# Weights converted ahead during MLP 1 and kept in DRAM, and full-height score matmuls for the first pair, in a fused attention, MLP and SoLU-MLP kernel

## The chip, the cores and the metric

The kernel runs on one core of one Trainium2 chip, as one launch. The metric is device time in microseconds. The kernel before took 1009.99 us (median of 3 runs, 1005.29 to 1010.61). Its profiled execution took 1004.9 us, of which 1003.1 us lie between its first and last instruction (the span).

## The reference

Three layers follow one another, in float32 results from inputs that numpy hands over partly in float64 (the MLP weights):

```python
# attention: q, k, v (4, 12, 448, 64)
q_n, k_n = rmsnorm(q, g_q), rmsnorm(k, g_k)          # over the 64 columns of a head
attn = softmax(q_n @ k_n.T / 8)                      # 448 x 448 per head, 48 heads
x = (attn @ v), heads side by side                   # (1792, 768)
# MLP 1: w_in (768, 2048), w_out (2048, 768)
h = x @ w_in;  x = (h * sigmoid(h)) @ w_out
# MLP 2: w_in (768, 1024), w_out (1024, 768)
h = x @ w_in;  solu = h * softmax(h)                 # softmax over the 1024 columns
ln = (solu - mean) / sqrt(var + 1e-6) * g_ln;  out = ln @ w_out
```

## The kernel before, in words

**Precision and weights.** The matmuls of both MLPs run in a 32-bit format (`F32R`) in which a value is kept as a high part and a low part. Each product is three matmuls: high with low, low with high, high with high. The weights arrive as float64, two 32-bit words each, and are converted on the chip. `stages` does that for one chunk (128 partitions x 384 weights) in eight steps: `load` (a DMA of the raw words by SP's queue into `raw`), `mag` (ACT, into `cva`), `clamp`, `shift`, `sign`, `low` (four DVE instructions, into `cva` and `cvt`), `hi` (ACT writes the high part) and `lo` (POOL writes the low part as `cvt` minus high). For the last weight matrix ACT also multiplies by `g_ln`, twice a chunk. A slab is four chunks with both parts, 12,288 bytes a partition. There are 24 slabs: 16 for MLP 1 (a `w_in` and a `w_out` for each of 8 groups of 256 hidden units) and 8 for MLP 2. The buffers `raw`, `cva` and `cvt` are threefold during the MLPs.

**Room.** Slabs live in two pools: `big` (10 places, 8 of them taken by the attention's output `xt` until MLP 1 has read it) and `big2` (2 places, odd groups). MLP 2's eight slabs fit only when the places of `xt` come free, batch by batch, in the last group of MLP 1.

**Attention.** 24 pairs of heads, each with 7 score tiles of 128 x 448. A greedy planner (`timetable`) with costs and ranks sets the order on all engines. A pair's queries are split into a high part `X` (`hq`, POOL) and a low part `lz` (`lq`). Of pair 0 (`DIRECT`) the scores of a head are two matmuls over 64 partitions and one over 128; other pairs get their operands stacked by DMAs (`Z`, `bd`). Before pair 0 come its own RMS chain (`ldk`, `sqk`, `redk`, `lnk`, `exk`, `nwk`, `sck`), the transposes `Tk`, and `hk` and `lk`, which make the high and low keys from PSUM with the gains `gsc`. `warm(n)` issues n matmuls of the identity.

**MLP 1.** 32 steps, one for a group of weights and a batch of 448 tokens: part a (36 matmuls into `hp`, then two SiLU evaluations on ACT and a difference on POOL into `gt`) and, one step later, part b (36 matmuls into six `xps` tiles, each added to the running sum `x` by one DVE instruction). Part b has six PSUM buffers, part a two.

**The order of conversions.** The programme is written out in order; each engine runs its instructions in that order. `enqueue` gives every step of a chunk a due time on a clock that advances by 1.13 for each 6 matmuls, `every` apart from chunk to chunk, and `tick` issues what is due between the matmuls. `EV` holds the spacings: 6.8 for groups 2 to 6, 2.4 for the last group, 2.1 and 2.3 for MLP 2's weights, which are queued at the four steps of the last group and run on into the first tiles of MLP 2.

**MLP 2.** 14 tiles of 128 tokens: `moe2_a` (36 matmuls into `h2`), the softmax and norm on DVE and ACT (`moe2_n`), transposes (`lp`) and `moe2_b` (48 matmuls). `split` makes high and low parts of `x`. The first `moe2_a` comes before MLP 1's last part b, and tile 0's softmax steps lie between the additions of that part on DVE.

Of the kernel before, what the change touches and what calls it, by code (L numbers as in the profile page):

```python
# [9 lines left out]
F32 = mybir.dt.float32  # L10
# [83 lines left out]
def fused_kernel(ctx: ExitStack, tc, nat, qt, gqk, w_in, w_out, w2_in, w2_out, g_ln, out):  # L94
# [13 lines left out]

    def stages(w, src, g, ph, c):

# [37 lines left out]
        def hi():  # L148
            k["hi"], k["lo"] = w()[:, 0, s], w()[:, 1, s]
            if g is None:  # L150
                nc.scalar.copy(out=k["hi"], in_=k["tf"])  # L151
            else:
                nc.scalar.activation(out=k["hi"], in_=k["tf"], func=AF.Identity, scale=g[:, c // 2:c // 2 + 1])
                if LO[ph] == "p":
                    nc.scalar.activation(out=k["tf"], in_=k["tf"], func=AF.Identity, scale=g[:, c // 2:c // 2 + 1])

        def lo():
# [43 lines left out]
    lz = [a1.tile([128, 2 * S], F32R, name=f"lz{i}") for i in range(2)]  # L201

    def constants():
# [6 lines left out]
        for t in bd + lz:  # L210
            nc.gpsimd.memset(t[:, :].bitcast(F32), 0.0)

    def gains():
        nc.sync.dma_start(out=gcol[:, :], in_=gqk)
        nc.sync.dma_start(out=gln[:, :], in_=g_ln)

# [17 lines left out]
    def attention(n):  # L234

        b, j = pairs[n]
        c, st_ = {}, {}

        def step(f):
# [112 lines left out]
        def hq():  # L352
            nc.gpsimd.tensor_scalar(out=X()[:, 0, 64:512], in0=c["qT"][:, :], scalar1=1.0, scalar2=0.0,
                                    op0=ALU.mult, op1=ALU.add)

        def lq(h):
            r = slice(64 * h, 64 * h + 64)
            en[LQE[h]].tensor_tensor(out=lz[n % 2][r, h * S:(h + 1) * S], in0=c["qT"][r, :],
                                     in1=c["X"][r, 0, 64:512].bitcast(F32), op=ALU.subtract)

# [25 lines left out]
        def mixed(h):  # L386
# [13 lines left out]
        def score(i):  # L400
            h, t = TILES[i]
            sp = c["sp"][i] = ps_s.tile([128, S], F32, name="sp", tag="sp")
            x, z = c["X"], lz[n % 2]
            if h == 2:
                mm = [(z[:, 384:512], x[:, 1, keys(0)]), (bd[n % 2][:, :], x[:, 2, keys(0)]),
                      (bd[n % 2][:, :], x[:, 1, keys(0)])]
            else:
                r, q = slice(64 * h, 64 * h + 64), 64 * h + t * 128
                mm = [(z[:, h * S + q:h * S + q + 128], x[:, 1, keys(h)])]
                if n in DIRECT:  # L410
                    mm = [(x[r, 0, 64 + q:192 + q], x[r, w, keys(h)]) for w in (1, 2)] + mm
# [150 lines left out]
    def spec(n):  # L562
# [26 lines left out]
        put("Tk", "PE", .63, LP, "sck", ["ks", ("t", "T")])  # L589
        put("hq", "p", .56, L, "ldT", "qT X")  # L590
        put("hk", "a", .57, L, "Tk", [("t", "T"), "X"])
        put("lk", "v", .66, L, "hk", [("t", "T"), "X"])
        for h in "01":
            put("lq" + h, LQE[int(h)], 1.1 if LQE[int(h)] == "p" else .7, L, "hq", "qT X lz")
            if n not in DIRECT:
                put("za" + h, "SP", moved(S), LD, "hq hk", "X Z")
                put("zb" + h, "SP", moved(S), LD, "hq lk", "X Z")
            put("b" + h, "SP", moved(0), LD, "hq", "X bd")
        for i, (h, t) in enumerate(TILES):
            s = ("sp", i)  # L600
# [66 lines left out]
    for c, f in enumerate([x[2] for x in sorted(due, key=lambda x: x[1])]):  # L667
# [370 lines left out]
```

## Time and profile before

| | us |
|---|---|
| median of 3 runs (lowest, highest) | 1009.99 (1005.29, 1010.61) |
| profiled execution | 1004.9 |
| its span | 1003.1 |
| PE busy | 982.5 |
| DVE, ACT, POOL busy | 665.6, 448.0, 407.7 |

Attention takes the first 280 us, MLP 1 runs from there to about 761 us, and MLP 2 to the end. PE is the engine to read: a wait of PE is lost time unless something later absorbs it. In a row of the timeline the bracket at the end names the idle time before the instruction and what ended it. The rows of PE show matmuls of 448 columns that start 0.2 us apart and are each shown some 0.37 us long, since they are pipelined; steps are therefore measured from start to start.

### The profile page before, as it was taken

The page shows a single profiled execution, that of the slowest core. Times are in us where ns is not written, and L with a number is a line of the kernel's source. Part 1 is how long each engine was busy: PE and PEld are TensorE (multiplying, and loading weights), DVE is VectorE, ACT ScalarE, POOL GpSimd, SP SyncE. Part 2 cuts the span into 40 slices and gives each one's busy share as a digit, 9 for nine tenths or more (in the row PEclk, how much of TensorE's full clock was granted, in tenths as well). Part 3 has the DMA queues.
Part 4 walks back from the last instruction along what each step waited for, and adds up shares of the span by engine and source line. Part 5 has one row for each costly group of instructions (what it writes and reads, how often), then busy time and mean ns, then how long its engine had stood idle before and what let it go on. Part 6 is the DMA issues. An engine that isn't in the chain of part 4 may idle for free. (4 is left out here: it accounts for less than half of the span.)

```text
span 1003.1 us, 14589 instructions
## 1 busy us (share of the span) xinstructions
PE 982.5 (98%) x5070; PEld 831.9 (83%) x5070; DVE 665.6 (66%) x1319; ACT 448.0 (45%) x1054; POOL 407.7 (41%) x577
## 2 busy tenths in 40 slices
PE   7999999999999999999999999999898999999998
PEld 5666756666789999999999999999886999989998
DVE  6899898888546555555555655989999653535431
ACT  5999989988732322222222232333554221212221
POOL 6978888878333322322332232444543110100000
PEclk9999999999999999999999999999999999999999
DMA  6776767765322121212112121344431000000001
GB/s 183 213 194 180 203 176 208 192 188 133 99 63 64 50 62 48 64 48 63 48 48 63 48 63 49 110 110 111 126 96 47 16 32 17 17 31 16 32 16 48
DMA packets 42472, 89.68 MB, mean 89 GB/s; under 512 B 8544, under 2 KB 20704, under 8 KB 42400
## 3 DMA queue, kind: packets, MB, share of 16 engines
q1 hardware_dynamic: 42400, 88.76, 31.7%
q8 instruction: 40, 0.66, 0.3%
q14 instruction: 32, 0.26, 0.1%
HBM read 61.35 MB, written 5.51 MB: 67 GB/s over the span
## 5 line engine op out<-in xcount | busy, mean ns | idle before, releaser
L729 PE MATMUL hp<-xt,slab 128*128 128x448 f32 x1152 | 242.9, 368 | 2.8 <-ACT gt L736 2.8
L752 PE MATMUL xps<-gt,slab 128*128 128x448 f32 x1152 | 241.4, 367 | 3.6 <-DVE x L758 3.6
L729 PEld LDWEIGHTS hp<-xt,slab 128*128 128x128 f32 x1152 | 217.3, 189 | 24.1 <-ACT gt L736 3.2
L752 PEld LDWEIGHTS xps<-gt,slab 128*128 128x128 f32 x1152 | 217.2, 189 | 22.7 <-DVE x L758 4.6
L163 POOL TENSOR_TENSOR slab<-cvt,slab 128x384 fp32r<-128x384 f32 x96 | 101.6, 1061 | 195.7 <-ACT slab L151 166.5
L758 DVE TENSOR_TENSOR x<-xps,x 128x448 f32<-128x448 f32 x168 | 102.8, 621 | 69.7 <-PE xps L752 69.7
L151 ACT CAST slab<-cvt 128x384 fp32r<-128x384 f32 x80 | 41.3, 516 | 224.9 <-DVE cvt L145 224.9
L737 POOL TENSOR_TENSOR gt<-gf,gt 128x448 fp32r<-128x448 f32 x64 | 74.9, 1172 | 128.8 <-ACT gt L736 95.1
L423 DVE TENSOR_SCALAR_CACHE_REDUCE sp<-sp,ms 128x448 f32<-128x448 f32 x168 | 110.3, 686 | 19.7 <-PE sp L415 19.6
L921 PE MATMUL op<-slab,lt 128*128 128x384 f32 (+2 forms) x672 | 120.8, 338 | 0.0
L921 PEld LDWEIGHTS op<-slab,lt 128*128 128x128 f32 x672 | 117.6, 188 | 2.1
L848 PE MATMUL h<-slab,xh 128*128 128x512 f32 x504 | 118.0, 392 | 0.8 <-DVE x L758 0.8
L848 PEld LDWEIGHTS h<-slab,xh 128*128 128x128 f32 x504 | 93.7, 188 | 20.0 <-issue 1.1
L459 POOL TENSOR_SCALAR p<-p,st 128x448 f32<-128x448 f32 x144 | 94.4, 665 | 28.9 <-DVE st L450 23.6
L133 DVE TENSOR_SCALAR cva<-cva 128x384 f32<-128x384 f32 x96 | 58.7, 612 | 68.1 <-ACT cva L130 68.1
L434 ACT ACTIVATE p<-sp,st 128x448 f32<-128x448 f32 x144 | 92.3, 642 | 15.0 <-DVE sp L423 12.4
L476 PE MATMUL tp<-ident,p 128*128 128x128 f32 x504 | 79.3, 275 | 1.9 <-ACT ht L494 1.5
L476 PEld LDWEIGHTS tp<-ident,p 128*128 128x128 f32 x504 | 60.3, 140 | 25.2 <-ACT ht L494 9.4
L881 POOL TENSOR_SCALAR sm<-sm 128x1 f32<-128x1 f32 x14 | 2.9, 205 | 189.8 <-DVE sm L880 189.8
L494 ACT COPY ht<-tp 128x384 f32<-128x384 f32 (+1 forms) x144 | 73.2, 530 | 6.8 <-PE tp L476 3.0
L508 PE MATMUL pv<-ht,vn 128*64 128x448 f32 x288 | 69.6, 564 | 0.0
L141 DVE SCALAR_TENSOR_TENSOR cvt<-raw,cva 128x384 uint32<-128x384 uint32 x96 | 65.4, 681 | 6.0
(105 smaller groups left out, 1223.0 us busy)
## 6 DMA issues: line engine op xcount, KB each, us to landing
Z<-X SPq DMA_DIRECT2D x92, 224.0 KB, 3.7
raw<-w_in SPq DMA_DIRECT2D x48, 384.0 KB, 3.1
raw<-w_out SPq DMA_DIRECT2D x48, 384.0 KB, 3.1
nat<-nat SPq DMA_DIRECT2D x23, 480.0 KB, 4.1
vn<-nat SPq DMA_DIRECT2D x24, 256.0 KB, 3.6
qT<-qt SPq DMA_DIRECT2D x24, 224.0 KB, 2.7
y<-ob SPq DMA_DIRECT2D x13, 384.0 KB, 2.3
bd<-X SPq DMA_DIRECT2D x48, 16.0 KB, 2.6
```

The source lines that it names most:

```text
L163: en[LO[ph]].tensor_tensor(out=k["lo"], in0=tf, in1=h, op=ALU.subtract)
L423: nc.vector.tensor_scalar(out=sp, in0=sp, scalar1=c["ms"][:, g:g + 1], scalar2=None, op0=ALU.mult, op1=ALU.min, accum_out=c["st"][:, 0, i: ...
L434: nc.scalar.activation(out=P(i), in_=c["sp"][i][:, :], func=AF.Exp, bias=c["st"][:, 0, i:i + 1], scale=-1.0, accum_out=c["st"][:, 1, i:i + 1])
L459: nc.gpsimd.tensor_scalar(out=p, in0=p, scalar1=r, scalar2=0.0, op0=ALU.mult, op1=ALU.add)
L476: nc.tensor.transpose(tp[:, o + t * 128:o + (t + 1) * 128], p[:, a:a + 128], ident[:, :])
L494: nc.scalar.copy(out=c["ht", kt][:, o], in_=src)
L729: nc.tensor.matmul(hp[0][:, 0:S], ws[g][0][:, pw, kd * 256 + m * 128:kd * 256 + (m + 1) * 128], xT[(b, kd)][:, px, :], start=(i == 0), sto ...
L737: nc.gpsimd.tensor_tensor(out=gt[0][:, 1, m, :], in0=gf[:, :], in1=gt[0][:, 0, m, :].bitcast(F32), op=ALU.subtract)
L752: nc.tensor.matmul(xps[:, 0:S], ws[g][1][:, pw, m * 768 + d * 128:m * 768 + (d + 1) * 128], gt[0][:, px, m, :], start=(j == 0), stop=(j == 5))
L758: nc.vector.tensor_tensor(out=x2[b][:, d, :], in0=xps[:, 0:S], in1=x2[b][:, d, :], op=ALU.add)
L848: nc.tensor.matmul(h2[:, half, :], xh[:, px, kd, :], wt[:, pw, (kd % 3) * 512:(kd % 3 + 1) * 512], start=(i == 0), stop=(i == 3 * KD - 1))
L921: nc.tensor.matmul(op[:, 0:c1 - c0], lt[:, px, k, :], wt[:, pw, o + c0:o + c1], start=(i == 0), stop=(i == 23))
```

## The change

Conversions are moved, the first pair's scores are built otherwise, and the start is reordered.

1. The weights of MLP 1's last group and of MLP 2, ten slabs, are no longer converted when their places come free. While groups 1 to 5 run, each group's queue takes, behind the two slabs of the next group, two of these ten. Their high and low parts are written over `cva` and `cvt` and stored by two DMAs a chunk into DRAM tiles (`park`). Spacing is 3.55 for all chunks instead of 6.8, and the load stands 4.5 ahead of the first step instead of 3.0. When a place comes free, `unpark` loads a finished slab with two DMAs.
2. For pair 0 the high queries go to `hz`, a zeroed tile with each head on its own half of the partitions, and every score is three matmuls over all 128 partitions, preceded by one identity matmul (`IDLE`). `hq` becomes `hq0` and `hq1`, both `lq` go to POOL, and pair 0's two small DMAs (`bd`) go.
3. The gains are loaded by ACT's queue at the very start, `gsc` is computed behind `sck`, and the identity matmuls are 17 and 7 instead of 12 and 4.

```diff
 def stages(w, src, g, ph, c, park=None):
         def hi():
+            if park is None:
-            k["hi"], k["lo"] = w()[:, 0, s], w()[:, 1, s]
+                k["hi"], k["lo"] = w()[:, 0, s], w()[:, 1, s]
+            else:
+                k["hi"], k["lo"] = k["a"].bitcast(F32R), k["t"].bitcast(F32R)
...
+        def store(i):
+            nc.sync.dma_start(out=park[:, i, s], in_=(k["af"], k["tf"])[i])
...
     def gains():
-        nc.sync.dma_start(out=gcol[:, :], in_=gqk)
+        nc.scalar.dma_start(out=gcol[:, :], in_=gqk)
...
+            if n in DIRECT:
+                hi = hz[0][:, q:q + 128]
+                mm += [(hi, x[:, 2, k]), (hi, x[:, 1, k])]
+                for _ in range(IDLE):
+                    nc.tensor.matmul(sp[:, 0:128], ident[:, :], ident[:, :], start=True, stop=True)
...
-    STEP = (0, 3.0, 4.2, 4.8, 5.4, 6.0, 7.2, 8.4)
+    STEP = ((0, 3.0, 4.2, 4.8, 5.4, 6.0, 7.2, 8.4), (0, 4.5, 5.7, 6.3, 6.9, 7.5, 8.7, 9.9, 9.9, 11.5))
...
+    def unpark(pool, keep, park):
+        t = slab(pool)
+        for i in range(2):
+            nc.sync.dma_start(out=t[:, i, :].bitcast(F32), in_=park[:, i, :])
+        keep.append(t)
...
-    NW = (12, 4)
+    NW = (17, 7)
...
-    EV = (6.8, 5.5, 2.4, 2.1, 2.3)
+    EV = (3.55, 5.5)
...
         if b == 0 and 0 < g < NMG - 2:
-            flow.append((0, lambda g=g: fetch(g + 1, EV[0])))
+            def ahead(g=g):
+                fetch(g + 1, EV[0])
+                for x in range(2 * g - 2, 2 * g):
+                    enqueue(None, [], parked[x][0], EV[0], parked[x][1], ph=2 if x < 6 else 3, park=parks[x])
+            flow.append((0, ahead))
+        if g == NMG - 2 and b < 2:
+            flow.append((0, lambda b=b: unpark(P_["big2"], ws[NMG - 1], parks[b])))
...
         if g == NMG - 1:
             def fetch2(b=b):
-                for i in range(2 * b, 2 * b + 2):
...
+                for x in range(2 * b + 2, 2 * b + 4):
+                    unpark(big, w2, parks[x])
```

The first place is DVE in the middle of MLP 1, about one step of one batch. The `cva` and `cvt` rows are the four instructions of a chunk, the `x` rows add one `xps` tile each. Before:

```order
L758 TENSOR_TENSOR x_1_3775<-xps,x_1_3775 128x448
L141 SCALAR_TENSOR_TENSOR cvt<-raw,cva 128x384
L145 SCALAR_TENSOR_TENSOR cvt<-raw,cvt 128x384
L758 TENSOR_TENSOR x_1_3775<-xps,x_1_3775 128x448 x5
L133 TENSOR_SCALAR cva<-cva 128x384
L137 TENSOR_SCALAR cva<-cva 128x384
L141 SCALAR_TENSOR_TENSOR cvt<-raw,cva 128x384
L145 SCALAR_TENSOR_TENSOR cvt<-raw,cvt 128x384
```

The same stretch of such a step now:

```order
L800 TENSOR_TENSOR x_3_3805<-xps,x_3_3805 128x448
L142 SCALAR_TENSOR_TENSOR cvt<-raw,cva 128x384
L146 SCALAR_TENSOR_TENSOR cvt<-raw,cvt 128x384
L800 TENSOR_TENSOR x_3_3805<-xps,x_3_3805 128x448 x2
L134 TENSOR_SCALAR cva<-cva 128x384
L138 TENSOR_SCALAR cva<-cva 128x384
L800 TENSOR_TENSOR x_3_3805<-xps,x_3_3805 128x448
L142 SCALAR_TENSOR_TENSOR cvt<-raw,cva 128x384
L146 SCALAR_TENSOR_TENSOR cvt<-raw,cvt 128x384
L800 TENSOR_TENSOR x_3_3805<-xps,x_3_3805 128x448 x2
```

A whole chunk more stands between the six additions of a step, and nearly two between one step's additions and the next's.

The second place is DVE where MLP 1's last part b meets tile 0 of MLP 2: `sm` and `gt` are tile 0's softmax, `x_3` the last batch's sum. Before:

```order
L137 TENSOR_SCALAR cva<-cva 128x384
L860 TENSOR_REDUCE sm<-h_7676 128x2
L861 TENSOR_TENSOR sm<-sm 128x1
L758 TENSOR_TENSOR x_3_3777<-xps,x_3_3777 128x448
L781 TENSOR_TENSOR xh<-x_0_3615,xh 128x768
L141 SCALAR_TENSOR_TENSOR cvt<-raw,cva 128x384
L145 SCALAR_TENSOR_TENSOR cvt<-raw,cvt 128x384
L133 TENSOR_SCALAR cva<-cva 128x384
L758 TENSOR_TENSOR x_3_3777<-xps,x_3_3777 128x448
L868 TENSOR_SCALAR sm<-sm 128x1
```

Now:

```order
L800 TENSOR_TENSOR x_3_3805<-xps,x_3_3805 128x448 x6
L903 TENSOR_REDUCE sm<-h_7885 128x2
L904 TENSOR_TENSOR sm<-sm 128x1
L800 TENSOR_TENSOR x_3_3805<-xps,x_3_3805 128x448
L823 TENSOR_TENSOR xh<-x_0_3631,xh 128x768
L800 TENSOR_TENSOR x_3_3805<-xps,x_3_3805 128x448
L911 TENSOR_SCALAR sm<-sm 128x1
```

No conversion is left between them, nor in the 36 additions ahead of this place.

The third place is SP's queue in MLP 1, where before only `raw` loads stood. Now, for two chunks:

```order
L170 DMA park_3634<-cva 128x384
L123 DMA raw<-w_out 128x768
L170 DMA park_3634<-cvt 128x384
L170 DMA park_3635<-cva 128x384
L123 DMA raw<-w_out 128x768
```

Between two loads stand a store that waits for POOL's `lo` and one that waits for ACT's `hi`.

## Rows read from the trace of the kernel before

**Rows 1.** The page's head: the span, then busy time of each engine.

```profile
span 1003.1 us, 14589 instructions
PE 982.5 (98%) x5070; PEld 831.9 (83%) x5070; DVE 665.6 (66%) x1319; ACT 448.0 (45%) x1054; POOL 407.7 (41%) x577
```

**Rows 2.** Timeline of PE, end of MLP 1: start, length, instruction, [idle before, releaser].

```profile
698.27 7.51 PE L752 MATMUL xps<-gt,slab 128*128 128x448 f32 x36
708.63 9.13 PE L729 MATMUL hp<-xt,slab 128*128 128x448 f32 x36 [2.84 <-ACT gt L736]
...
740.49 8.46 PE L848 MATMUL h<-slab,xh 128*128 128x512 f32 x36 [0.76 <-DVE x L758]
748.78 5.03 PE L752 MATMUL xps<-gt,slab 128*128 128x448 f32 x24
757.24 2.51 PE L752 MATMUL xps<-gt,slab 128*128 128x448 f32 x6 [3.42 <-DVE x L758]
...
761.67 8.37 PE L848 MATMUL h<-slab,xh 128*128 128x512 f32 x36
771.02 1.09 PE L897 MATMUL lp<-ident,gt 128*128 128x128 f32 x8 [0.98 <-DVE gt L886]
771.87 3.44 PE L848 MATMUL h<-slab,xh 128*128 128x512 f32 x14
```

**Rows 3.** Windows: stretch, length, busy time (instructions) by engine, clock, DMA.

```profile
345.00:605.00 260.00, 260.00 (x1281) 240.13 (x1280) 145.06 (x251) 67.84 (x140) 76.69 (x71) 1.00 0.19 54
625.00:700.00 75.00, 75.00 (x371) 69.30 (x370) 68.21 (x114) 29.15 (x61) 33.48 (x31) 1.00 0.40 110
700.00:775.00 75.00, 66.77 (x303) 57.76 (x302) 69.96 (x117) 37.99 (x72) 32.95 (x30) 0.95 0.33 91
```

**Rows 4.** Groups by line, 625 to 700 us: count, busy us, mean ns, idle.

```profile
L163 POOL TENSOR_TENSOR slab<-cvt,slab 128x384 fp32r<-128x384 f32 x22 | 24.1, 1101 | 27.2 <-ACT slab L151 24.7 <-PE hp L729 2.5
...
L758 DVE TENSOR_TENSOR x<-xps,x 128x448 f32<-128x448 f32 x28 | 17.3, 618 | 4.4 <-PE xps L752 4.4
```

**Rows 5.** Timeline of DVE in the middle of MLP 1.

```profile
344.99 1.02 DVE L133 TENSOR_SCALAR cva<-cva 128x384 f32<-128x384 f32 x1 [3.04 <-ACT cva L130]
...
350.80 0.62 DVE L758 TENSOR_TENSOR x<-xps,x 128x448 f32<-128x448 f32 x1 [0.44 <-PE xps L752]
...
353.77 0.35 DVE L133 TENSOR_SCALAR cva<-cva 128x384 f32<-128x384 f32 x1
...
355.43 0.56 DVE L141 SCALAR_TENSOR_TENSOR cvt<-raw,cva 128x384 uint32<-128x384 uint32 x1
```

**Rows 6.** Timeline of POOL in the same stretch.

```profile
344.64 1.15 POOL L737 TENSOR_TENSOR gt<-gf,gt 128x448 fp32r<-128x448 f32 x1 [1.06 <-issue]
...
350.45 1.02 POOL L163 TENSOR_TENSOR slab<-cvt,slab 128x384 fp32r<-128x384 f32 x1 [1.04 <-ACT slab L151]
```

**Rows 7.** Timeline of all engines at the start.

```profile
1.34 5.37 PE L225 MATMUL tp<-ident 128*128 128x128 f32 x24 [1.34 <-POOL ident masks.py:199]
...
5.21 0.21 ACT L318 ACTIVATE y<-y 128x8 f32<-128x8 f32 x1
...
7.92 0.21 DVE L218 TENSOR_SCALAR gsc<-gcol 128x1 f32<-128x1 f32 x1 [2.62 <-DMA gcol<-gqk]
...
9.52 0.69 DVE L288 TENSOR_TENSOR ks<-nat,ms 128x512 f32<-128x512 f32 x1
...
10.27 0.90 PE L346 MATMUL tp<-ident,ks 128*128 128x128 f32 x3 [3.56 <-DVE ks L288]
...
13.24 0.68 PE L415 MATMUL sp<-X 64*128 64x448 f32 x2
...
16.16 0.49 PE L346 MATMUL tp<-ident,ks 128*128 128x128 f32 x3
```

**Rows 8.** DMA issues: form, count, KB each, median us to landing.

```profile
Z<-X SPq DMA_DIRECT2D x92, 224.0 KB, 3.7
...
y<-ob SPq DMA_DIRECT2D x13, 384.0 KB, 2.3
```

More of the change, by code (lines that the diff above doesn't have):

```diff
@@ L163, in lo @@
                 en[LO[ph]].tensor_tensor(out=k["lo"], in0=tf, in1=h, op=ALU.subtract)
-        return [load, mag, clamp, shift, sign, low, hi, lo]
+        def store(i):
+            nc.sync.dma_start(out=park[:, i, s], in_=(k["af"], k["tf"])[i])
+        return [load, mag, clamp, shift, sign, low, hi, lo] + \
+            ([lambda: store(0), lambda: store(1)] if park is not None else [])
     en = {"v": nc.vector, "p": nc.gpsimd}
@@ L209, in constants @@
                                     op=ALU.add)
-        for t in bd + lz:
+        for t in lz + bd:
             nc.gpsimd.memset(t[:, :].bitcast(F32), 0.0)
+        hz.append(big.tile([128, 2 * S], F32R, name="hz", tag="big"))
+        nc.vector.memset(hz[0][:, :].bitcast(F32), 0.0)
     def gains():
-        nc.sync.dma_start(out=gcol[:, :], in_=gqk)
-        nc.sync.dma_start(out=gln[:, :], in_=g_ln)
+        nc.scalar.dma_start(out=gcol[:, :], in_=gqk)
+        nc.scalar.dma_start(out=gln[:, :], in_=g_ln)
     def gain():
@@ L237, in attention @@
         c, st_ = {}, {}
+        lqe = LQ0 if n in DIRECT else LQE
         def step(f):
@@ L354, in hq, with hq_ @@
                                     op0=ALU.mult, op1=ALU.add)
+        def hq_(h):
+            r = slice(64 * h, 64 * h + 64)
+            nc.gpsimd.tensor_scalar(out=hz[0][r, h * S:(h + 1) * S], in0=c["qT"][r, :], scalar1=1.0,
+                                    scalar2=0.0, op0=ALU.mult, op1=ALU.add)
         def lq(h):
-            r = slice(64 * h, 64 * h + 64)
-            en[LQE[h]].tensor_tensor(out=lz[n % 2][r, h * S:(h + 1) * S], in0=c["qT"][r, :],
-                                     in1=c["X"][r, 0, 64:512].bitcast(F32), op=ALU.subtract)
+            r, o = slice(64 * h, 64 * h + 64), slice(h * S, (h + 1) * S)
+            hi = hz[0][r, h * S:(h + 1) * S] if n in DIRECT else c["X"][r, 0, 64:512]
+            en[lqe[h]].tensor_tensor(out=lz[n % 2][r, o], in0=c["qT"][r, :], in1=hi.bitcast(F32), op=ALU.subtract)
         @step
@@ L589, in spec @@
         put("Tk", "PE", .63, LP, "sck", ["ks", ("t", "T")])
-        put("hq", "p", .56, L, "ldT", "qT X")
+        if n not in DIRECT:
+            put("hq", "p", .56, L, "ldT", "qT X")
         put("hk", "a", .57, L, "Tk", [("t", "T"), "X"])
@@ L593, in spec @@
         for h in "01":
-            put("lq" + h, LQE[int(h)], 1.1 if LQE[int(h)] == "p" else .7, L, "hq", "qT X lz")
-            if n not in DIRECT:
+            if n in DIRECT:
+                put("hq" + h, "p", .4, L, "ldT sck", "qT")
+                put("lq" + h, LQ0[int(h)], .9 if LQ0[int(h)] == "p" else .56, L, "hq" + h, "qT lz")
+            else:
+                put("lq" + h, LQE[int(h)], 1.1 if LQE[int(h)] == "p" else .7, L, "hq", "qT X lz")
                 put("za" + h, "SP", moved(S), LD, "hq hk", "X Z")
                 put("zb" + h, "SP", moved(S), LD, "hq lk", "X Z")
-            put("b" + h, "SP", moved(0), LD, "hq", "X bd")
+                put("b" + h, "SP", moved(0), LD, "hq", "X bd")
         for i, (h, t) in enumerate(TILES):
             s = ("sp", i)
-            if h == 2:
+            if n in DIRECT:
+                put(f"s{i}", "PE", .62 + .22 * IDLE, LP, ("lq0 lq1" if h == 2 else f"lq{h}") + " hk lk", [s, "X", "lz"])
+            elif h == 2:
                 put(f"s{i}", "PE", .6, LP, "b0 b1 lq0 lq1 hk lk", [s, "X", "lz", "bd"])
-            elif n in DIRECT:
-                put(f"s{i}", "PE", 1.0, LP, f"lq{h} hk lk", [s, "X", "lz"])
             else:
@@ L677, in fused_kernel @@
     D_ = 1e-5
-    g0 = max(at[0, "ldq"], at[0, "ldk"], at[1, "ldqk"]) + D_
     ops = [(at[k], i, f) for i, (k, f) in enumerate(ops.items())]
-    NW = (12, 4)
-    ops += [(-1000, 0, constants), (-999, 0, lambda: warm(NW[0])), (g0, 0, gains),
-            (max(g0, at[0, "redq"]) + D_, 0, gain), (at[0, "Tk"] + D_, 0, lambda: warm(NW[1]))]
+    NW = (17, 7)
+    ops += [(-1001, 0, gains), (-1000, 0, constants), (-999, 0, lambda: warm(NW[0])),
+            (at[0, "sck"] + D_, 0, gain), (at[0, "Tk"] + D_, 0, lambda: warm(NW[1]))]
     E_LAST = max(at[N - 1, f"e{i}"] for i in range(7)) + D_
@@ L708, in fused_kernel @@
     HL = [(0, 1), (1, 0), (0, 0)]
+    dram = ctx.enter_context(tc.tile_pool(name="park", bufs=1, space=bass.MemoryType.DRAM))
+    parked = [(w_in[NMG - 1], None), (w_out[NMG - 1], None)] + [(w2_in[i], None) for i in range(4)] + \
+        [(w2_out[i], gln[:, 2 * i:2 * i + 2]) for i in range(4)]
+    parks = [dram.tile([128, 2, SLAB], F32, name=f"park{i}") for i in range(len(parked))]
     def fetch(g, every=6.8):
```

36 lines of the change are left out of this document (16 added, 20 removed), and 2 rows, old and new, of the table RANK.

## The prediction

> **What bounds the kernel now.** I read the page's head first: PE is busy for 982.5 of 1003.1 us [rows 1], so the other engines matter only where they make PE wait or let its clock fall. The windows show where that is: in the middle of MLP 1 PE is busy for all 260 us, from 700 to 775 us only for 66.77 of 75, and there the granted clock is 0.95 [rows 3]. PE's timeline names the waits [rows 2]: 2.84 us for ACT at 708 us, 0.76 and 3.42 us for DVE's `x` at 740 and 757 us, 0.98 us for DVE's norm at 771 us. In that stretch DVE is busy for 69.96 of 75 us, against 145.06 of 260 us in the middle [rows 3]; what it has more to do are the conversions queued at 2.1 to 2.4 spacing.
>
> What this costs PE is read from start to start. From 698.27 to 771.87 us are 73.60 us [rows 2]. In them stand six MLP 1 halves of 36 matmuls, two `moe2_a` and eight transposes. Undisturbed, 1281 matmuls take 260 us [rows 3], so 36 take 7.31. A `moe2_a` takes 8.37, the transposes 0.85 (771.87 less 771.02) [rows 2]. 6 x 7.31 + 2 x 8.37 + 0.85 = 61.45. So 12.1 us are lost: 8.2 in waits (75 less 66.77 [rows 3]; the four named are 8.0), the rest in matmuls at the lower clock level, as in the 9.13 us of the half at 708.63 us, whose like takes 7.51 [rows 2].
>
> **The change, part by part.** *End of MLP 1.* All conversions leave DVE, ACT and POOL there; the order shows `x`, the peak and tile 0's softmax behind one another. The waits for `x` and ACT go with them. Next late could be tile 0's norm, 0.98 us before. With the additions at 0.62 each and no chunk between, DVE catches up while PE does 7.31 + 8.37 us of other work, so I leave 0.5 us. Gain 11.6 us; at least about half of it, at most 12.1.
>
> *The slabs' way back.* Twenty loads of 0.79 MB replace conversions. MLP 2 first needs `w2_out` some 45 us after its last slab's place comes free (the last part a ends a part b, 7.31 us, before the `moe2_a` of 740.49: 733 us; `moe2_b` follows the `moe2_a` of 771.87, at 780 us [rows 2]). The nearest rows move 110 GB/s [rows 3], so two slabs (3.1 MB) take at most 29 us. Hidden, 0. If a load were late PE would wait whole microseconds, once.
>
> *Groups 1 to 5.* 80 chunks are added there, and the 40 of the next groups move closer. A step of PE is 2 x 7.31 = 14.62 us and advances the clock by 13.56, so 3.55 is 3.83 us: 3.82 chunks a step. Free, a chunk takes DVE 2 x 0.35 + 2 x 0.56 = 1.82 us [rows 5], POOL 1.02, and each of a step's two differences 1.15 [rows 6]. The `clamp` at 344.99 us took 1.02 instead of 0.35 while POOL worked until 345.79, and the addition at 350.80 beside POOL's `lo` of 350.45 kept its 0.62 [rows 5, 6]. So DVE's conversion steps and POOL shut each other out, additions don't. A step thus needs 3.82 x (1.82 + 1.02) + 2 x 1.15 = 13.1 of 14.62 us, 90%. The Trainium skill says the same in SBUF — State Buffer, Who interferes with whom: a DVE instruction with two SBUF inputs, or in a 2-port mode, is blocked for the whole of a POOL instruction that reads SBUF, and one with a single SBUF input isn't. By that rule the addition, which has one input in PSUM, stays outside the sum; were it inside, 13.1 + 6 x 0.62 = 16.8 us would not fit 14.62 and each step would be 2.2 us longer. The rows agree with the rule.
>
> The test is in the trace: from 625 to 700 us DVE ran 22 chunks in 75 us [rows 4], one each 3.41 us, and PE was busy for all 75 [rows 3]. But only 28 additions ran [rows 4] where 371 matmuls, half of them in part b, give 371 / 72 x 6 = 31, so it was slipping by 3 x 0.62 = 1.9 us: the pace that could last is about 3.41 x 76.9 / 75 = 3.50. The new pace of 3.83 leaves 9%. I take no wait of PE. From both sides: 0, or, since each 0.1 us by which a chunk is slower than 3.83 costs 80 x 0.1, 8 us for each such tenth. A bound above comes from strict turns of 16.8 us a step: 21 steps x 2.2 = 46 us. I stay near the row at 3.50.
>
> *The stores.* They are new; the nearest rows are output stores, 2.3 us for 384 KB, and `Z`, 3.7 us [rows 8]. `cva` is due for its store at 9.9 and for its next chunk's `mag` at 4.5 + 3 x 3.55 = 15.15, that is 5.25 x 14.62 / 13.56 = 5.7 us later; `cvt` from 11.5 to 17.55, 6.5 us. At 2.3 to 3.7 us to landing, 2 us or more are left. Bytes: a chunk loads and stores 393 KB each, 786 KB in 3.83 us or 205 GB/s; 110 GB/s took a share of 0.40 [rows 3], so this takes about 0.75 of the DMA engines. Behind a store that waits in SP's queue stands the next `raw` load, which has a lead of 4.5. I take 0; a loss comes as a slower pace, priced above.
>
> *Start.* `gsc` held DVE for 2.62 us on the gains' DMA [rows 7]. With `gsc` behind `sck`, `nwk` can start when ACT's `ex` ends at 5.42. From `gsc` at 7.92 to `ks` at 9.52 are 1.60 us [rows 7], of which pair 0's second `lq` (now on POOL; over 448 columns, as an addition, 0.6 [rows 5]) and `gsc` (0.2) leave, so `ks` runs from about 6.2 to 6.9. PE stands in front: 12 identity matmuls are 24 records in 5.37 us [rows 7], 17 end between 7.8 (if the last ten records run at double clock) and 8.95. `Tk` so starts 1.3 to 2.5 us before the 10.27 of now, and without the idle 3.56 us before it at the clock of the later `Tk`, 0.49 instead of 0.90 for the first three [rows 7]. But POOL now has two `hq` and two `lq` of pair 0 to do before pair 1's Newton steps, so pair 1 gains less than pair 0. PE is near full from then on, so what pair 1 gains counts. I take 1.5 us; bounds are -1 and 3.5. The full-height scores issue as many score matmuls as before; their 7 identity matmuls and the larger warm-up stand where PE waits for `lk` or before.
>
> **Sum.** 1004.9 - 11.6 - 1.5 = 991.8 us, against the profiled execution. The median of the runs shown is 1009.99, their lowest 1005.29; 13.1 us off the median are 996.9. Between these two I name 994; its own range is 987 to 1000.
>
> **Rivals.**
> - *Conversion becomes the bound of MLP 1 (slower).* Place: DVE's queue in groups 1 to 5, where an addition stands behind a chunk that waits for POOL, a load or a store's buffer; PE then waits in part b for an `xps` buffer. It decides when the lasting pace passes 3.83 + 13.1 / 80 = 3.99 us. At 4.1: 80 x 0.27 = 21.6, and 994 + 21.6 = 1016. For it: DVE and POOL already 90% taken by turns, stores not in the trace, no pause between groups, since 16 x 3.55 = 56.8 exceeds the 54.24 of a group. Against it: 3.50 lasted.
> - *The same, mild.* Pace 3.91: 80 x 0.08 = 6.4, so 1000.
> - *The wait at the end isn't the conversions'.* Tile 0's peak and softmax stand before the additions on DVE in both orders. If that chain holds PE, the 12.9 us from 748.78 to 761.67 [rows 2], 5.6 above 7.31, stay about as they are: 994 + 5 = 999. Against it: the additions late at 757 us stood behind conversions and a peak that was itself late.
>
> **How the numbers follow.** Forecast 0.55, slower rival 0.14, mild one 0.16, the end's wait 0.15. About 0.5%, 5 us, is what a measurement of this kernel can tell from no change. Faster by more: nearly all of the forecast (0.53), 0.09 of the mild one, 0.11 of the end's wait: 0.73. Within 0.5%: 0.02 + 0.06 + 0.04 and 0.03 of the slower rival: 0.15. Slower: 0.12, the rest. The range of 986 to 1008 holds the forecast, the two middle rivals and the weakest part of the slower one.
>
> **What would show it.** Right: PE busy throughout 620 to 775 us with clock 1.00, 22 to 23 us of DVE in each 25 us of groups 1 to 5 and no wait of PE there, the first score near 11 us, MLP 2 as long as before. Wrong: waits of PE for `x` or `gt` in groups 1 to 5, steps longer than 14.7 us, ACT's `mag` or DVE's `sign` waiting for a store, PE waiting for a slab from DRAM, or a first pair that starts earlier with an attention that ends no sooner.

## The result and the profile after

The changed kernel took 992.09 us (median of 6 runs, 991.02 to 994.03), the kernel before 1010.3 beside it (6 runs, 1005.02 to 1011.14): a ratio of 0.9835, 95% interval 0.9813 to 0.9857. The profiled execution took 991.99 us with a span of 990.0; before's took 1004.9 with 1003.1. The forecast was 994.0.

The head of the page, against [rows 1]:

```profile
span 990.0 us, 14963 instructions
PE 979.4 (99%) x5100; PEld 834.2 (84%) x5100; DVE 661.6 (67%) x1319; ACT 448.2 (45%) x1054; POOL 411.2 (42%) x579
```

PE does about the same work in 13.1 us less span. PE's timeline at the end of MLP 1, which answers to [rows 2] (L794, L771, L891 and L940 are before's L752, L729, L848 and L897):

```profile
697.49 7.50 PE L794 MATMUL xps<-gt,slab 128*128 128x448 f32 x36
704.83 7.59 PE L771 MATMUL hp<-xt,slab 128*128 128x448 f32 x36
...
734.37 8.38 PE L891 MATMUL h<-slab,xh 128*128 128x512 f32 x36
742.58 7.46 PE L794 MATMUL xps<-gt,slab 128*128 128x448 f32 x36
749.88 8.35 PE L891 MATMUL h<-slab,xh 128*128 128x512 f32 x36
758.07 1.04 PE L940 MATMUL lp<-ident,gt 128*128 128x128 f32 x8
```

No row has a wait. From the part b at 697.49 to the transposes at 758.07 are 60.58 us; before, from 698.27 to 771.02, 72.75 [rows 2]. That is 12.2 of the 13.1 us. Another 0.8 is there already where the first full part a of MLP 1 begins, so it comes from the attention. Before, then now:

```profile
280.54 7.95 PE L729 MATMUL hp<-xt,slab 128*128 128x448 f32 x36
```

```profile
279.75 7.95 PE L771 MATMUL hp<-xt,slab 128*128 128x448 f32 x36
```

The windows of [rows 3] again:

```profile
345.00:605.00 260.00, 260.00 (x1280) 240.16 (x1279) 221.12 (x379) 104.01 (x213) 114.79 (x105) 1.00 0.52 151
625.00:700.00 75.00, 75.00 (x371) 69.29 (x370) 28.73 (x49) 18.25 (x36) 19.14 (x16) 1.00 0.48 173
700.00:775.00 75.00, 75.00 (x366) 67.22 (x365) 32.94 (x57) 10.99 (x24) 9.98 (x13) 1.00 0.18 70
```

DVE's work has moved: 221.12 us in the middle instead of 145.06, 32.94 at the end instead of 69.96. PE is busy in all three, with the clock at its upper level. DVE's groups by line in the middle (count, busy us, mean ns, idle before):

```profile
L800 DVE TENSOR_TENSOR x<-xps,x 128x448 f32<-128x448 f32 x108 | 66.2, 619 | 28.4 <-PE xps L794 28.0
L142 DVE SCALAR_TENSOR_TENSOR cvt<-raw,cva 128x384 uint32<-128x384 uint32 x68 | 53.4, 785 | 3.5
...
L134 DVE TENSOR_SCALAR cva<-cva 128x384 f32<-128x384 f32 x68 | 38.2, 561 | 4.0 <-ACT cva L131 3.9
```

The addition (L800) keeps its 0.62 us on average; the conversion's `sign` (L142) takes 0.79 for 0.56 and its `clamp` (L134) 0.56 for 0.35 [rows 5], since part of each is spent shut out by POOL. By the Trainium skill (SBUF — State Buffer, Who interferes with whom) a DVE instruction with at most one SBUF input, outside the 2-port modes, isn't blocked; the mean of these 108 additions, whose other input is in PSUM, agrees. (The `clamp` has one SBUF input as well and is slowed; no row here names its mode.)

28.0 us of DVE's idle time are spent waiting for PE: DVE is ahead. The new transfers, beside [rows 8]:

```profile
slab<-park SPq DMA_DIRECT2D x20, 768.0 KB, 6.2
park<-cva SPq DMA_DIRECT2D x40, 192.0 KB, 1.9
park<-cvt SPq DMA_DIRECT2D x40, 192.0 KB, 3.3
```

The start on PE, against [rows 7]:

```profile
1.34 6.81 PE L239 MATMUL tp<-ident 128*128 128x128 f32 x34 [1.34 <-POOL ident masks.py:199]
7.99 0.49 PE L360 MATMUL tp<-ident,ks 128*128 128x128 f32 x3
...
10.25 0.45 PE L439 MATMUL sp<-X,lz 128*128 128x448 f32 x1
...
14.52 0.55 PE L360 MATMUL tp<-ident,ks 128*128 128x128 f32 x3 [0.49 <-POOL ks L302]
...
21.28 0.71 PE L439 MATMUL sp<-Z 128*128 128x448 f32 x1 [2.45 <-DMA Z<-X]
```

The first score is 3.0 us earlier (13.24 before), pair 1's `Tk` 1.6 us (16.16 before), and then PE waits 2.45 us for pair 1's `Z`. Behind that wait the clock drops, 0.50 on average from 21 to 24 us:

```profile
21.00:24.00 3.00, 2.72 (x10) 2.47 (x11) 2.72 (x8) 2.24 (x6) 3.00 (x4) 0.50 0.98 208
```

### The profile page after: what moved, and what is told of

Same layout as the page of the kernel before. It is cut to its first block, busy times and chain, and to the rows that moved or that the text cites. A ratio compares the mean times of both kernels' runs of the same rounds, so it can differ in the third digit from the quotient of the medians.

```text
span 990.0 us, 14963 instructions
## 1 busy us (share of the span) xinstructions
PE 979.4 (99%) x5100; PEld 834.2 (84%) x5100; DVE 661.6 (67%) x1319; ACT 448.2 (45%) x1054; POOL 411.2 (42%) x579
## 4 chain that ended last, share of the span: by engine, by line
PE 93%; DVE 2%; POOL 2%; ACT 2%; issue 1%; DMA 1%; DVEq 0%; POOLq 0%; ACTq 0%
PE hp L771 24%; PE xps L794 24%; PE op L964 12%; PE h L891 12%; PE sp L439 6%; PE pv L532 6%; PE tp L500 5%; PE pv L535 2%; PE lp L940 1%; DVE sp L447 1%; PE tp L360 1%; ACT p L458 1%; PE tp L505 1%; POOL lz L379 0%; POOL p L483 0%
## 5 line engine op out<-in xcount | busy, mean ns | idle before, releaser
L771 PE MATMUL hp<-xt,slab 128*128 128x448 f32 x1152 | 241.4, 367 | 0.0
L794 PE MATMUL xps<-gt,slab 128*128 128x448 f32 x1152 | 239.6, 366 | 0.0
L771 PEld LDWEIGHTS hp<-xt,slab 128*128 128x128 f32 x1152 | 216.1, 188 | 20.8 <-issue 2.2
L794 PEld LDWEIGHTS xps<-gt,slab 128*128 128x128 f32 x1152 | 216.4, 188 | 18.1
L800 DVE TENSOR_TENSOR x<-xps,x 128x448 f32<-128x448 f32 x168 | 103.1, 620 | 93.8 <-PE xps L794 93.2
L891 PE MATMUL h<-slab,xh 128*128 128x512 f32 x504 | 117.9, 392 | 0.0
L891 PEld LDWEIGHTS h<-slab,xh 128*128 128x128 f32 x504 | 93.7, 188 | 18.8
L458 ACT ACTIVATE p<-sp,st 128x448 f32<-128x448 f32 x144 | 92.5, 643 | 13.6 <-DVE sp L447 10.0
L777 ACT ACTIVATE gf<-hp 128x448 f32<-128x448 f32 x64 | 34.8, 544 | 129.7 <-PE hp L771 128.5
L167 POOL TENSOR_TENSOR slab<-cvt,slab 128x384 fp32r<-128x384 f32 x56 | 59.5, 1063 | 70.2 <-ACT slab L155 65.6
L500 PEld LDWEIGHTS tp<-ident,p 128*128 128x128 f32 x504 | 60.2, 140 | 24.6 <-ACT ht L518 12.1
L142 DVE SCALAR_TENSOR_TENSOR cvt<-raw,cva 128x384 uint32<-128x384 uint32 x96 | 70.7, 736 | 6.2 <-DMA park<-cvt 1.4
L167 POOL TENSOR_TENSOR cvt<-cvt,cva 128x384 fp32r<-128x384 f32 x40 | 44.1, 1102 | 63.1 <-issue 19.8
L155 ACT CAST slab<-cvt 128x384 fp32r<-128x384 f32 x56 | 29.0, 517 | 91.2 <-DVE cvt L146 91.0
```

The costliest lines, as they stand in the source:

```text
L458: nc.scalar.activation(out=P(i), in_=c["sp"][i][:, :], func=AF.Exp, bias=c["st"][:, 0, i:i + 1], scale=-1.0, accum_out=c["st"][:, 1, i:i + 1])
L500: nc.tensor.transpose(tp[:, o + t * 128:o + (t + 1) * 128], p[:, a:a + 128], ident[:, :])
L771: nc.tensor.matmul(hp[0][:, 0:S], ws[g][0][:, pw, kd * 256 + m * 128:kd * 256 + (m + 1) * 128], xT[(b, kd)][:, px, :], start=(i == 0), sto ...
L794: nc.tensor.matmul(xps[:, 0:S], ws[g][1][:, pw, m * 768 + d * 128:m * 768 + (d + 1) * 128], gt[0][:, px, m, :], start=(j == 0), stop=(j == 5))
L800: nc.vector.tensor_tensor(out=x2[b][:, d, :], in0=xps[:, 0:S], in1=x2[b][:, d, :], op=ALU.add)
L891: nc.tensor.matmul(h2[:, half, :], xh[:, px, kd, :], wt[:, pw, (kd % 3) * 512:(kd % 3 + 1) * 512], start=(i == 0), stop=(i == 3 * KD - 1))
```

## The experiments

**1 and 2: each part alone.** `e_start` has the start and the first pair of the change, with before's conversions; `e_park` the moved conversions, with before's start.

```diff
 # e_start
-EV = (3.55, 5.5)
+EV = (6.8, 5.5, 2.4, 2.1, 2.3)      # and before's STEP, flow and fetch2, no DRAM tiles
...
 # e_park
-NW = (17, 7)
+NW = (12, 4)                        # and before's gains, gsc and pair 0's scores
```

> Start and first pair of the change, conversions as before. Theory (the gain is the conversions' and stands at the end of MLP 1): the first full part a of MLP 1 begins some 0.8 us earlier than before (at about 279.8 instead of 280.5), the waits of PE for `gt` and `x` after 700 us and the 12 us lost there stay: span about 1002.3, ratio to before 0.997 to 1.000. Rival (the start carries a good part, for example through an attention that runs in another order): span 998 or less.

Measured: 1005.5 us (1004.22 to 1008.35), ratio to before 0.9965 [0.9948, 0.9983]. The theory held for the place of the waits: at the end of MLP 1 PE waits 7.7 us for `gt` and `x`, the longest two on its timeline:

```profile
711.02 10.05 PE L766 MATMUL hp<-xt,slab 128*128 128x448 f32 x36 [3.03 <-ACT gt L773]
...
759.74 1.68 PE L789 MATMUL xps<-gt,slab 128*128 128x448 f32 x6 [3.43 <-DVE x L795]
```

It did not hold for the start. The profiled execution is the slowest of the ten, its span is 1006.6 us, and its first full part a begins at 282.25 us, 2.5 later than the change's: PE's wait ahead of pair 1's `Z` is 3.71 us there, and from 24 to 28 us the clock is 0.62 on average. That the start is worth 4.6 us rests on the medians alone.

> Conversions moved and kept in DRAM, start and first pair as before. Theory: 12.2 us less, all between the last part b's and tile 1 of MLP 2, span about 990.9, ratio 0.985 to 0.989. Rival: 4 us less or under, if the start is needed for the rest.

Measured: 997.09 us (996.37 to 997.31), ratio 0.9893 [0.9861, 0.9926], and no wait of PE behind 620 us. So the conversions are 13.0 us of the gain by medians (1010.12 less 997.09), and the start is 4.6 (1010.12 less 1005.5) to 5.0 (997.09 less 992.09), not the 0.8 that the two profiles show. Its own profile shows where this start loses time. PE's timeline at the start, and the window behind it:

```profile
9.89 0.90 PE L353 MATMUL tp<-ident,ks 128*128 128x128 f32 x3 [4.00 <-DVE ks L295]
...
12.86 1.11 PE L422 MATMUL sp<-X 64*128 64x448 f32 x2
```

```profile
13.00:28.00 15.00, 15.00 (x34) 9.15 (x35) 9.37 (x21) 7.85 (x19) 5.54 (x12) 0.50 0.52 137
```

With the same start as before, but 4.00 us of idle time ahead of `Tk` where before's profile has 3.56 [rows 7], the clock is at its lower level, 1.2 GHz, through all of pair 0, and a pair of half-height scores takes 1.11 us where [rows 7] has 0.68. Before's single runs fall in two groups, near 1005 (10 of 40) and near 1010, and the profiled one, 1004.9, is of the rarer. That the 1010 are executions with this slow pair 0 fits their granted clock over the whole span (0.984 to 0.988, against 0.993 to 0.995), but no profile of before shows one, so this is argued and not shown.

**3: a pace that cannot last.** The change with the conversions of groups 1 to 5 due at every 2.4.

```diff
-EV = (3.55, 5.5)
+EV = (2.4, 5.5)
```

> The changed kernel with chunks 2.4 apart instead of 3.55 (2.59 us instead of 3.83), same work in each group, then a pause. Theory (DVE and POOL, which shut each other out, last at about 3.50 us a chunk; beyond that the additions fall behind, and PE waits once they are about half a step, 7.3 us, late): 16 chunks need 56 us where 41.4 are given, so PE waits 56 - 41.4 - 7.3 = 7 us in each of five groups, 20 to 45 us more than the changed kernel, 1012 to 1037 us, with waits for `x` or ACT's `gt`. Rival (PE waited at the end of MLP 1 because of tile 0's softmax and of the places that came free there, not because of the pace): no change, 990 to 994.

Measured: 1015.38 us (1013.59 to 1016.87), 23 more than the change and a little more than before: 1.0069 [1.004, 1.0099]. PE's waits by cause (us in total, times, longest), and the first of them on its timeline:

```profile
PE hp L771 <- ACT gt L778: 15.7, 8, 4.4
```

```profile
387.95 9.99 PE L771 MATMUL hp<-xt,slab 128*128 128x448 f32 x36 [4.41 <-ACT gt L778]
```

All are for ACT's `gt`, none for DVE's `x`; behind them matmuls run at the lower clock (9.99 us for a half that takes 7.50). ACT's `mag` from 345 to 640 us shows what held ACT:

```profile
L131 ACT ACTIVATE cva<-raw 128x384 f32<-128x384 f32 x76 | 41.9, 552 | 66.1 <-DMA park<-cva 37.9 <-issue 13.1 <-DMA raw<-w_in 8.2
```

It waits for the store that must free `cva` (37.9 us), whose median landing is now 3.7 us instead of 1.9; the SiLU stands behind `mag` in ACT's order. In the changed kernel the same line, from 345 to 605 us, idles 5.5 us and never for a store.

So this run does not test the theory's limit alone. By the prediction's own working, `cva` has 5.7 us between its store and its next `mag` at 3.55; at 2.4 it has (4.5 + 3 x 2.4 - 9.9) x 14.62 / 13.56 = 1.9 us, less than the 3.7 that a store takes here. From 340 to 370 us, ahead of the first store of the burst, DVE is busy for 9.4 to 9.6 us in each 10 and the additions fall behind; where PE stands waiting it is busy for less:

```profile
380.00:390.00 10.00, 5.59 (x24) 4.78 (x23) 7.32 (x13) 4.69 (x10) 3.14 (x3) 0.81 0.60 200
```

DVE and POOL's turns and the way of the stores are both too slow for this pace, and the run does not tell what each costs.

**4: each store twice.** A second store of the same bytes to another DRAM tile.

```diff
 nc.sync.dma_start(out=park[:, i, s], in_=(k["af"], k["tf"])[i])
+nc.sync.dma_start(out=P_["twin"][:, i, s], in_=(k["af"], k["tf"])[i])
```

> The changed kernel with each store into DRAM issued twice, the second into a tile that nothing reads; loads and arithmetic as they are. Theory (stores are hidden, they land 2 us or more before their buffers are wanted): no wait of PE, 990 to 994 us, though the copies add 15.7 MB to MLP 1 and three DMAs of a chunk become five. Rival (the stores are near their limit: SP's queue and the buffers `cva` and `cvt`): ACT's `mag` and DVE wait for landings, PE for additions, over 997 us.

Measured: 992.26 us (991.6 to 992.81). Window and landing times:

```profile
345.00:605.00 260.00, 260.00 (x1280) 240.15 (x1279) 220.66 (x379) 104.92 (x213) 115.21 (x105) 1.00 0.64 200
```

```profile
park<-cva SPq DMA_DIRECT2D x40, 192.0 KB, 3.1
```

200 GB/s instead of 151 and landings of 3.1 us instead of 1.9 change nothing for PE, which waits for nothing from 280 to 700 us. DVE does wait for landings there, 11.4 us in all against 1.4 in the change; at the spacing of 3.55 the stores are hidden with room.

**5: half-height scores with the rest of the start.** `e_park` with the early gains, `gsc` behind `sck`, and 17 and 7 identity matmuls.

```diff
-NW = (12, 4)
+NW = (17, 7)
...
-(g0, 0, gains), (max(g0, at[0, "redq"]) + D_, 0, gain)
+(-1001, 0, gains), (at[0, "sck"] + D_, 0, gain)     # gains on ACT's queue
```

> e_park with two thirds of the new start: gains on ACT's queue, `gsc` behind `sck`, 17 and 7 identity matmuls; pair 0's scores stay half-height. Theory (e_park's start is long because PE's clock stands at its lower level while pair 0's half-height matmuls run, from 8 to 28 us in its profile, and rises only behind them): the clock may still stand low through pair 0, in some executions or all, median 994 to 998, first part a of MLP 1 some 1 to 5 us later than the changed kernel's 279.75. Rival (the early gains and the longer warm-up did it): 991 to 993, first part a at 280 or before.

Measured: 990.1 us (989.69 to 990.62), ratio 0.9814 [0.9787, 0.9842]. The theory that half-height scores keep the clock low fell; the gain is larger than the rival's, and the first full part a begins at 277.57 us. PE's timeline, and the window to set against that of `e_park`:

```profile
8.74 0.55 PE L353 MATMUL tp<-ident,ks 128*128 128x128 f32 x3 [1.52 <-DVE ks L295]
...
11.01 0.67 PE L422 MATMUL sp<-X 64*128 64x448 f32 x2
...
20.15 0.44 PE L422 MATMUL sp<-Z 128*128 128x448 f32 x1 [1.28 <-ACT p L441]
```

```profile
13.00:28.00 15.00, 12.55 (x63) 8.71 (x63) 14.44 (x40) 13.65 (x38) 11.04 (x23) 1.00 0.81 221
```

`Tk` is later than in the change (8.74, 7.99) and the first score of `Z` is earlier (20.15, 21.28). POOL makes one `lq` of pair 0 there instead of two and comes to pair 1's norm at 10.88 instead of 11.47 us; pair 1's `Tk` starts at 13.92, 14.52 in the change.

**6, 7 and 8: pieces of the full-height start.** The change without pair 0's identity matmuls (`e_idle0`), with 12 and 4 of the others (`e_nw12`), and with pair 1's `lk` ahead of pair 2's reduction and pair 3's load behind pair 1's `Z` (`e_lk_nat`).

```diff
 # e_idle0
-LQ0, IDLE = "pp", 1
+LQ0, IDLE = "pp", 0
 # e_nw12
-NW = (17, 7)
+NW = (12, 4)
 # e_lk_nat
+at[1, "lk"] = at[2, "red"] - D_
+at[3, "ldqk"] = max(at[1, "zb1"], at[1, "za1"]) + D_
```

> The changed kernel without the identity matmul ahead of each of pair 0's scores. Theory (full-height matmuls keep the clock up by themselves): 991 to 994, first score tile as before or 0.2 us earlier each. Rival (the identity matmuls fill the pauses between the scores, and the clock needs them): clock 0.50 during pair 0's scores in its profile, median 994 to 998.

Measured: 991.17 us (990.64 to 991.47): without them it is some 1 us faster than the change, not slower. In its profile the clock is 1.00 through pair 0's scores and falls behind them (0.74 from 16 to 21 us, 0.50 from 21 to 24).

> The changed kernel with 12 and 4 identity matmuls at the start instead of 17 and 7. Theory (what counts is pair 0's full-height scores): 991 to 994; the pause of PE before `Tk` grows from none to 1 us. Rival (the clock must be up before the scores, and 12 don't bring it up): clock 0.50 from about 10 us for some us, 993 to 997.

Measured: 992.02 us (991.82 to 993.4): no difference. PE waits 1.37 us ahead of `Tk`, and the clock stays at 1.00 up to 21 us, as in the change.

> The changed kernel with two instructions of the start elsewhere: pair 1's low keys (`lk`) stand before pair 2's sum of squares on DVE, and pair 3's load of 480 KB behind pair 1's four `Z` DMAs on SP's queue. Theory (pair 0's gain of 3 us is lost because pair 1's `Z` come late: `lk` ended at 18.1 us, 2.1 us behind `hk`, and a load went ahead): PE's wait for `Z` falls from 2.45 to about 1.2 us, first part a 0.5 to 1.3 us earlier than 279.75. Rival (the queue's issue time of 1 us a DMA, or a wait behind pair 2's, sets it): no change, or PE waits as much for pair 2's.

Measured: 995.32 us (995.04 to 996.41), ratio 0.9868 [0.9844, 0.9892]. A miss. PE's wait for `Z` ends 0.8 us sooner, but the load that was put back now lands late, ACT's exponentials stand behind the square of it, and PE behind those; from 24 to 28 us the clock is 0.50. ACT's and PE's timelines:

```profile
24.46 1.00 ACT L270 ACTIVATE qk<-nat 128x960 f32<-128x960 f32 x1 [3.28 <-DMA nat<-nat]
...
26.13 0.74 PE L439 MATMUL sp<-Z 128*128 128x448 f32 x1 [2.47 <-ACT pm L458]
```

**9 and 10: early gains alone, longer warm-up alone**, each on `e_park`: the one has the gains' lines of experiment 5, the other its `NW` line.

> The kernel with the conversions moved and the start of before (997.09), with one thing changed in the start: the gains travel on ACT's queue at the very start and `gsc` stands behind `sck` on VectorE; 12 and 4 identity matmuls and half-height scores as before. Theory (the early gains are the whole gain of the start: PE no longer idles 4.0 us ahead of the first `Tk`, so its clock does not fall): PE's idle time ahead of the first `Tk` is under 2.5 us, the clock is at its upper level from about 6 us, median 989 to 992. Rival (the longer warm-up is needed as well, since 12 identity matmuls end some 1.5 us earlier than 17): a wait of over 2.5 us remains ahead of `Tk`, the lower level lasts into pair 0's scores, median 994 to 997.5.

Measured: 995.58 us (992.0 to 996.79).

> The same base (997.09), with only the identity matmuls changed: 17 ahead of the first `Tk` and 7 behind it in place of 12 and 4; the gains travel late, as before. Theory (the gains decide): the first `hk` still waits for `gsc`, the first score stays at 13 us or later; PE's idle time ahead of `Tk` is some 1.5 us shorter, which keeps the clock up in some executions, median 993 to 997. Rival (PE's idle time ahead of `Tk` is all that matters, the gains only go along): the clock is at its upper level through pair 0 and the median is 989 to 992.5.

Measured: 994.01 us (991.96 to 998.02). PE's timelines, the early gains first:

```profile
8.58 0.55 PE L353 MATMUL tp<-ident,ks 128*128 128x128 f32 x3 [2.17 <-DVE ks L295]
```

```profile
9.84 0.55 PE L353 MATMUL tp<-ident,ks 128*128 128x128 f32 x3 [3.04 <-DVE ks L295]
```

In both profiles the clock is at its lower level from pair 0's first score on (1.11 us for a half-height pair), though before's profile, with a longer wait of 3.56 us, has it back at the upper level by then. So the length of this wait does not settle it alone. My theory, that the early gains do it all, fell: each piece shortens the idle time ahead of `Tk` (4.00 to 2.17 and to 3.04) and takes 1.5 to 3 us off the median, with a wide spread (the profiled execution of the longer warm-up is its slowest); the two together give 1.52 us of idle time and, in all five runs, under 991.

**11: pair 0's second `lq` behind `sck`**, on top of experiment 5.

```diff
+at[0, "lq1"] = at[0, "sck"] + 2 * D_
```

> The kernel of 990.1 (conversions moved, early gains, 17 and 7 identity matmuls, half-height scores), with pair 0's second `lq` moved behind `sck` and `gsc` on VectorE, where it stood ahead of both (7.34 to 8.00 us). Theory (VectorE's chain to the first `Tk` sets the start): `ks`, `Tk`, `hk` and the first score come 0.6 us earlier, 989.3 to 990. Rival (the `Z` transfers of pair 1, which PE waits for 6 us later, set the start, and they hang on pair 1's chain): nothing reaches the end, 989.8 to 990.6. A second rival: `lq` now stands ahead of pair 1's reduction, which makes pair 1 later by 0.6 us: 990.4 to 991.2.

Measured: 990.66 us (990.64 to 995.48). `Tk` comes 0.8 us earlier, at 7.98, and nothing reaches the end: three runs stand at 990.65, as the rival says. Of the other two the profiled one, at 993.5, lost the clock in pair 0 after all; the second, at 995.5, has no profile, and its granted clock over the span, 0.993, fits the same:

```profile
13.73 0.73 PE L353 MATMUL tp<-ident,ks 128*128 128x128 f32 x3 [0.29 <-POOL ks L295]
...
14.82 1.11 PE L422 MATMUL sp<-X 64*128 64x448 f32 x2
```

PE had been busy without a gap up to here, and waited only 0.29 us. What made the clock fall in this execution, I can't tell from the rows.

**12: a tighter pace that should last**, 3.0 instead of 3.55.

> The changed kernel (992.09) with its conversions in groups 1 to 5 at every 3.0 instead of 3.55 us by the counted clock, 3.23 us a chunk. The prediction's lasting pace was 3.50 us a chunk, so that each part a and b of a group falls behind by 16 x 0.27 = 4.3 us, under the half step of 7.3 us. Theory (VectorE recovers between the bursts, and a chain that is late by less than a step blocks nobody): no wait of PE for `x` or `gt` over 0.3 us, 991 to 993. Rival (the lag of one burst is carried into the next, as it was at 2.4): some waits for `gt` of 1 to 5 us in all, each with a stretch at the lower clock behind it, 995 to 1003.

Measured: 990.9 us (990.16 to 992.05), no wait of PE for `x` or `gt`. DVE's share of the middle:

```profile
345.00:605.00 260.00, 260.00 (x1281) 240.15 (x1280) 244.10 (x395) 109.31 (x225) 119.85 (x107) 1.00 0.56 161
```

DVE is at 244.10 of 260 us and PE still at 260. The difference to the change is within the two spreads. But DVE doesn't keep up. In one group, the first and the fourth part b on PE, and the first addition of each on DVE:

```profile
564.63 7.49 PE L794 MATMUL xps<-gt,slab 128*128 128x448 f32 x36
...
608.58 7.47 PE L794 MATMUL xps<-gt,slab 128*128 128x448 f32 x36
```

```profile
566.62 0.62 DVE L800 TENSOR_TENSOR x<-xps,x 128x448 f32<-128x448 f32 x1
...
614.09 0.62 DVE L800 TENSOR_TENSOR x<-xps,x 128x448 f32<-128x448 f32 x1
```

The addition comes 2.0 us behind the start of its part b, then 5.5; in the pause behind the 16 chunks it is back at 1.4 (623.19 and 624.61). In the change it is 1.4 or 1.5 us in every part b from 346 to 624 us. So 3.5 us are lost in 44 us, about as the theory says (4.3 in 16 chunks), and the pause makes them good. For bursts of 16 chunks with a pause behind them the bound lies between the paces of 3.0 and 2.4.

## Why the prediction was right

- **End of MLP 1: right.** 12.1 us were to be had and 11.6 were counted; 12.2 came. PE waits for nothing from 620 to 775 us, and the waits for `x` and `gt` return with the conversions (experiment 1) and go without them (experiment 2). The 0.5 left for tile 0's norm was not needed. The rival that tile 0's chain holds PE fell: the transposes at 758.07 wait for nothing.
- **The slabs' way back: right.** From its first transposes to the end of the span MLP 2 takes 231.9 us, 232.1 before (1003.1 less 771.02 [rows 1, 2]). A load lands in 6.2 us, so the four of two slabs take 24.8 even one behind another, under the 29 that were counted.
- **Groups 1 to 5: right in the time, wrong in the buffer.** DVE has 21.3 us in each 25 (221.12 of 260), where 22 to 23 were forecast; shut out by POOL it is, additions excepted, as counted. (40 of the 80 chunks there are added, not 80; the 3.82 chunks a step and the price of a tenth hold for all 80.) The lasting pace of 3.50 was about right: at 3.83 the additions never fall behind, at 3.23 they lose 3.5 us in 44 us, or 13.6 chunks, which gives an estimate of 3.23 + 3.5 / 13.6 = 3.5 (experiment 12). What fails first at a much closer pace isn't the `xps` buffer, which the slower rival named: PE stands at part a for `gt`, since ACT's `mag` waits for the store that frees `cva` and the SiLU stands behind it (experiment 3). At 3.0 that wait begins, 6.7 us of ACT's idle time from 345 to 605 us. The step followed the additions on DVE and left out what stands behind a conversion in ACT's order.
- **Stores: right.** Hidden from PE, and still hidden when doubled. Once, at 625.29 us, DVE's `sign` waits for a store, 1.39 us, and PE doesn't feel it. The 205 GB/s counted a store for every chunk; half of the chunks have none, and 151 were measured.
- **Start: the term that was mis-sized.** 1.5 us were taken. Between the two profiles nothing lasts: of the 3.0 us at the first score 1.0 is left at pair 1's first score of `Z` (22.30 before, 21.28 now), as the text feared ("pair 1 gains less than pair 0"), and 0.1 at the fifth pair's `Tk` (41.87, 41.81), the clock having dropped in between. The 0.8 at MLP 1 comes behind that, within what the later pairs vary by. By medians it is 4.6 to 5.0. The likely reason is that most executions of before lose PE's clock in pair 0, as `e_park` does with the same start; on before itself no trace shows it. The sum off the median, 996.9, was too high by 4.8, and the one off the profile, 991.8, right for the profile (991.99). The forecast of 994 was set between the two without a reason for the gap between profile and median; that it came within 2 us is in part luck.
- **Full-height scores: not free.** Experiment 5, without them and without the POOL work that they bring, is 2 us faster than the change. About 1 is the identity matmuls (experiment 6), which "stand where PE waits" only in part. By another count about 1 is the clock: behind the wait for pair 1's `Z` the change's profile loses it, and five of its six executions have a granted clock of 0.997 or 0.998 over the span, while the sixth, at 1.000, took 991.02 us and all five of experiment 5 stand at 1.000. In experiment 4, whose start is the same, the profile has the same wait of 2.45 us and keeps the clock:

```profile
21.00:24.00 3.00, 2.68 (x15) 2.19 (x15) 2.94 (x8) 2.65 (x7) 3.00 (x4) 1.00 0.99 222
```

Its two executions at 1.000 took 991.6 and 991.75 us, the two at 0.998 took 992.76 and 992.81. The two counts overlap, and no run separates them.

One doubt stands over differences of 1 us: the order of the attention's later pairs varies slightly from kernel to kernel, where the planner's ties fall another way, and from the fifth pair's `Tk` to the last one's took 200.4 to 202.3 us in the profiles. Experiment 5's lead is not of that kind: its fifth `Tk` is 2.2 us ahead of the change's.

The best version measured is that of experiment 5, at 990.1 us. Its five runs (989.69 to 990.62) lie below all six of the change (991.02 to 994.03), though not side by side on one chip. Whether full-height scores protect against a clock lost in pair 0 stays open: the 24 runs of the change and of experiments 4, 6, 7 and 12, all with full-height scores, lie between 990.2 and 994.0; of ten with half-height scores eight lie below 990.7 and two at 993.5 and 995.5.

## What to carry to other kernels

Work that is queued densely on a helper engine at the end of a stage can be spread over the stage before it, if that stage's own busy share, counted with the time in which engines shut each other out, leaves room; a trip through DRAM for the result cost PE nothing here. To find what breaks first when it doesn't fit, follow every engine and every buffer that the moved chain passes, in its queue's order, not only the busiest engine; a burst that is too dense is harmless as long as a pause behind it makes the lag good. And hold one profiled execution against the single runs: where these fall in two groups, a term read from the profile is right for one group only.

## What the runs showed of the hardware

PE's clock at the start was not the same in every execution, and the idle time ahead of the first real matmuls doesn't settle it alone. With 4.00 us of it the clock stayed at 1.2 GHz through the first pair (0.50 from 13 to 28 us, experiment 2), with 2.17 and 3.04 it was there from the first score on (experiments 9 and 10), and with 1.52 it stayed at 2.4 GHz (1.00, experiment 5). But before's profile, with 3.56, has it low from 10 to 13 us only (0.50, then 0.95 from 13 to 16), and in experiment 11 it fell in the midst of matmuls after a wait of 0.29 us. After the same wait of 2.45 us for `Z` it fell in the change's profile (0.50 from 21 to 24 us) and not in experiment 4's (1.00).

A store of 192 KB landed in 1.9 to 3.3 us (medians of the two kinds), in 3.1 to 4.3 when each was doubled, and in 2.7 to 3.7 at the pace of 2.4.
